# Attention and a softplus feed-forward on one core: block products in the first pass over d_ff for groups 4 and 5 too, and the softmax's scale after the product with v in the first group

## The chip, the core and the metric

One core of a Trainium2 chip runs the whole program. The metric is the device time of one execution in microseconds (us). The engines are TensorE (PE in the rows), VectorE (DVE), ScalarE (ACT), GpSimd (POOL) and SyncE (SP), which here does nothing but start DMAs.

## What is computed

```python
def _attn_ref(q, k, v):                       # B, H, S, D = 4, 8, 768, 64
    k_sum = k.reshape(B, H, nb, 32, D).max(axis=3)      # nb = 24 blocks of 32 keys
    v_sum = v.reshape(B, H, nb, 32, D).mean(axis=3)
    scores_l = scale * q @ k^T,   kept where abs(i - j) < 16
    scores_s = scale * q @ k_sum^T + log(32)
    a = softmax over [scores_l, scores_s]
    return a @ [v, v_sum]
def _moe_ref(x, w_in, w_out):                 # 3072 x 512, 512 x 2048, 2048 x 512
    h = x @ w_in
    return softplus(h) @ w_out
```

The output of the attention, with its heads side by side, is x. Everything is float32.

## The kernel before

**Tiling.** The 3072 tokens are 12 chunks of 256, and two chunks make a group of 512 tokens, so there are six groups, x = 0 to 5. d_ff = 2048 is 16 tiles of 128, f = 0 to 15. Phases follow one another: groups 0 to 4 with f = 0 to 7 (the first pass), group 5 with f = 0 to 15 at one stretch, then groups 4 to 0 with f = 8 to 15 (the second pass). A partial result of a group's first pass lies in DRAM until its second. The attention of group x + 1 is done while group x is in its first pass. Weights of f = 8 to 15 arrive, in the places of those of f = 0 to 7, while group 5 is worked on.

**Precision.** A float32 operand is split into a high and a low part that TensorE takes at its fast rate (float32r), and a product is three terms of those parts, so each product of 128 x 128 by some columns is three matmuls per tile of d_model.

**The two forms of x @ w_in.** `hidden(x, f)` is the plain one: four tiles of d_model by three terms, 12 matmuls of 512 columns into one PSUM bank. `hidden_pair(x, f)` does f and f + 1 together as a 2 x 2 block product with seven products in place of eight (tiles of d_ff by halves of the tokens by halves of d_model): each of the seven is 6 matmuls of 256 columns. It needs sums and differences of the blocks of w_in (`sums_of_weights`, buffers sw in places s0 to s3), sums and differences of the blocks of x (`prepare`: seven operands in places x0 to x6, of which x3 to x6 have one buffer), both banks that carry hidden values, and seven additions on VectorE. In the kernel before, `pairs = f0 > 0`: the second pass alone takes the pairs, and the first pass takes `hidden` on a group's x split whole (`prepare_whole`, `whole_x`).

Behind either form come, per f, ScalarE's softplus twice (gh, L1147, and the exact value, L1151), VectorE's rest gl (L1155), and 12 matmuls of 512 columns with w_out (L1162) into four banks.

**The first group's attention** has four blocks: chunk i (0, 1) by pair of heads hp (0, 2). Here they are called A (i 0, hp 0), B (i 1, hp 0), C (i 0, hp 2) and D (i 1, hp 2). For each, scores on TensorE (L629), mask and maximum on VectorE (L642), exp with sums on ScalarE (L650), the inverse of the sums (L657, L658), the scaling of the weights by it (`normalize`, on VectorE L663 for A and C, on ScalarE L666 for B and D), transposes on TensorE (L683), copies out of PSUM (L687), the product with v (L727), and from its bank the high and low parts of x (L757, L761). `keep_whole` adds these again later and writes them to DRAM for the second pass.

**Order.** Every operation is a task with an index, in the order in which the program declares them, and `SEQUENCE` says in which order the tasks are issued; a letter behind an index takes the task's second or third way (another engine). Each engine does its tasks in that order. In both kernels the tasks 3 to 42 are the warm-up, 43 to 63 loads and sums for the first batch, 153 to 245 the weights of f = 0 to 7, and 246 is the first product with w_in. Blocks A to D are the tasks 72 to 85, 86 to 99, 108 to 121, 122 to 135 before, and 72 to 88, 89 to 105, 114 to 130, 131 to 147 after the change.

## Time and profile before

| | |
|---|---|
| median of 3 runs | 631.66 us (630.81 to 633.7) |
| the profiled execution | 630.05 us |
| its span, first to last instruction | 628.3 us |
| mean granted TensorE clock | 0.983 of 2.4 GHz |
| HBM | 73.92 MB read, 27.26 MB written |

The span is what the trace shows; the profiled execution's own time is 1.75 us longer. A row of a group of instructions gives their line, engine, operation, tiles, shapes and count, then their busy time in us and the mean of one in ns, then the engine's idle time just before them and what ended it. Matmuls overlap one another, so the time that a row of them costs is read from start to start. "L1085" is a line of the program printed above.

### The profile page before, as it was taken

What the parts mean: (1) busy time and instruction counts of PE and PEld (TensorE: products, weight loads), DVE (VectorE), ACT (ScalarE), POOL (GpSimd) and SP (SyncE); (2) the same over time, 40 slices, a digit from 0 to 9 for tenths busy, and PEclk for the clock granted to TensorE, in tenths of its full rate; (3) what the DMA queues carried; (4) which work ended last, traced back from release to release, by engine and by line L of the source; (5) the groups of instructions that cost most, each with busy time, mean ns of one, the idle gap of its engine ahead of it and who ended that gap; (6) DMA issues with size and microseconds to landing.
All of it is one profiled execution on the core that took longest, in us unless ns stands there. A gap on an engine that the chain in (4) does not pass through costs nothing.

```text
span 628.3 us, 12022 instructions
## 1 busy us (share of the span) xinstructions
PE 609.2 (97%) x4452; PEld 508.9 (81%) x4452; DVE 388.0 (62%) x998; ACT 328.0 (52%) x809; POOL 162.0 (26%) x145
## 2 busy tenths in 40 slices
PE   8769999999999999999999999999999999999997
PEld 7557777788888878877888888899889899898995
DVE  5887997764457454535427979764557557655442
ACT  2898895965766676456526677441323122222220
POOL 3325435132213043002003443490111403002000
PEclk9868999999999999999999999999999999999999
DMA  9998887989998887885634632103122050030301
GB/s 303 265 272 268 254 264 233 262 261 231 272 263 253 259 268 220 254 236 158 212 116 155 222 127 84 34 34 118 51 76 78 17 185 1 35 100 1 104 32 67
DMA packets 88955, 104.39 MB, mean 166 GB/s; under 512 B 27489, under 2 KB 67009, under 8 KB 88129
## 3 DMA queue, kind: packets, MB, share of 16 engines
q1 hardware_dynamic: 88896, 103.62, 54.5%
q8 instruction: 35, 0.57, 0.4%
q14 instruction: 24, 0.19, 0.1%
HBM read 73.92 MB, written 27.26 MB: 161 GB/s over the span
## 4 chain that ended last, share of the span: by engine, by line
PE 85%; DMA 8%; SPq 3%; ACT 1%; DVE 1%; issue 1%; DVEq 0%; POOL 0%; POOLq 0%; ACTq 0%
PE po L1162 40%; PE ph L1045 21%; PE hx L1085 9%; PE hy L1085 7%; PE xo L727 3%; PE sc L629 3%; DMA raw<-w_in_dram 2%; DMA k<-kT_dram 2%; DMA squares<-tb 2%; PE warm L1236 2%; DMA kf<-kT_dram 1%; DMA q<-qT_dram 1%; DMA v<-v_hp_dram 1%; SPq L708 1%; SPq L523 1%
## 5 line engine op out<-in xcount | busy, mean ns | idle before, releaser
L1162 PE MATMUL po<-w,gh 128*128 128x512 f32 x768 | 204.2, 394 | 0.0
L1162 PEld LDWEIGHTS po<-w,gh 128*128 128x128 f32 x768 | 141.4, 188 | 30.6 <-issue 0.6
L1045 PE MATMUL ph<-xw,w 128*128 128x512 f32 x672 | 163.9, 395 | 2.1 <-DVE gl L1155 2.0
L1045 PEld LDWEIGHTS ph<-xw,w 128*128 128x128 f32 x672 | 125.6, 188 | 32.5 <-DVE gl L1155 2.8
L1162 PE MATMUL po<-w,gl 128*128 128x512 f32 x384 | 116.6, 397 | 0.0
L1162 PEld LDWEIGHTS po<-w,gl 128*128 128x128 f32 x384 | 70.9, 188 | 15.9 <-issue 0.5
L650 ACT ACTIVATE sp<-sp,nm 128x120 f32<-128x120 f32 x192 | 73.1, 382 | 5.9 <-DVE nm L642 5.7
L1147 ACT ACTIVATE gh<-hx 128x512 fp32r<-128x512 f32 x20 | 12.0, 599 | 114.9 <-DVE hx L1095 114.9
L948 POOL TENSOR_TENSOR t<-t,raw 128x1024 int32<-128x1024 int32 (+1 forms) x20 | 42.4, 2122 | 98.8 <-DVE t L934 28.4
L1155 DVE TENSOR_TENSOR gl<-ph,gh 128x512 fp32r<-128x512 f32 x56 | 38.0, 684 | 40.8 <-ACT ph L1151 39.3
L1147 ACT ACTIVATE gh<-ph 128x512 fp32r<-128x512 f32 x56 | 33.5, 598 | 53.4 <-PE ph L1045 48.5
L789 POOL TENSOR_TENSOR x<-r,x 128x512 fp32r<-128x512 f32 x18 | 24.5, 1370 | 82.0 <-ACT x L782 32.2
L642 DVE CUSTOM_DVE_ANT_0 sp<-sc,added 128x120 f32<-128x120 f32 x192 | 40.8, 277 | 4.9 <-PE sc L629 3.9
L663 POOL TENSOR_TENSOR sp<-sp,ss 128x960 f32<-128x960 f32 x10 | 18.4, 1843 | 87.6 <-DVE ss L658 62.8
L650 ACT ACTIVATION_READ_ACCUMULATOR sp<-sp,nm 128x1 f32 x192 | 36.0, 187 | 0.0
L1085 PE MATMUL hx<-x,sw 128*128 128x256 f32 x240 | 35.4, 283 | 0.0
L1085 PE MATMUL hx<-x,w 128*128 128x256 f32 x240 | 35.1, 282 | 0.0
L1085 PEld LDWEIGHTS hx<-x,w 128*128 128x128 f32 x240 | 32.8, 189 | 1.9
L696 DVE STREAM_TRANSPOSE tb<-sp 128x1024 f32<-128x1024 f32 x20 | 24.8, 1242 | 15.2 <-POOL sp L663 7.9
L1085 PE MATMUL hy<-x,sw 128*128 128x256 f32 x240 | 33.2, 282 | 0.0
L1151 ACT ACTIVATE ph<-ph 128x512 f32<-128x512 f32 x56 | 32.8, 591 | 0.0
L1085 PEld LDWEIGHTS hx<-x,sw 128*128 128x128 f32 x240 | 31.7, 189 | 0.5
(108 smaller groups left out, 821.6 us busy)
## 6 DMA issues: line engine op xcount, KB each, us to landing
squares<-tb SPq DMA_DIRECT2D x20, 512.0 KB
pT<-squares SPq DMA_DIRECT2D x80, 128.0 KB
raw<-w_out_dram SPq DMA_DIRECT2D x16, 512.0 KB
kf<-kT_dram SPq DMA_DIRECT2D x16, 384.0 KB
raw<-w_in_dram SPq DMA_DIRECT2D x6, 1024.0 KB
q<-qT_dram SPq DMA_DIRECT2D x20, 256.0 KB
raw<-r SPq DMA_DIRECT2D x20, 256.0 KB
part<-ob SPq DMA_DIRECT2D x10, 512.0 KB
```

Source lines behind the costliest of these rows:

```text
L629: nc.tensor.matmul(unit(g * NU + h * NPAIR + i)[r * QW:(r + 1) * QW, k0:k1], lhsT=q[rows, w * QW:(w + 1) * QW], rhs=k[rows], start=True, s ...
L642: nc.vector.tensor_tensor_reduce(out=sp()[:, n], in0=unit(n), in1=added()[:, kinds.index((lows[w], lows[w + 1]))], scale=-SCALE, scalar=FL ...
L650: nc.scalar.activation(sp()[:, n], sp()[:, n], AF.Exp, bias=nm()[:, n:n + 1], scale=-1.0, accum_out=ss()[:, n:n + 1],)
L696: nc.vector.transpose(out=tb().rearrange("p k (u q) -> p u k q", q=SQ), in_=tiles.sp().rearrange("p u (k q) -> p u k q", q=SQ),)
L789: engine.tensor_tensor(to(1), a(), to(0).bitcast(F32), op=ALU.subtract)
L948: nc.gpsimd.tensor_tensor(a, a, word(0, I32), op=ALU.add)
L1045: nc.tensor.matmul(ph(), lhsT=lhs(part, cc), rhs=xw[cc][0]()[:, xw[cc][1], a], start=cc == 0 and n == 0, stop=cc == NCC - 1 and n == 2,)
L1085: nc.tensor.matmul(to()[:, half], lhsT=lhs(wa, cc), rhs=of_x(xa)[:, cc * CH:(cc + 1) * CH], start=cc == 0 and m == 0, stop=cc == NG - 1 an ...
L1147: nc.scalar.activation(gh(), all_of(), AF.Softplus)
L1151: nc.scalar.activation(all_of(), all_of(), AF.Softplus)
L1155: nc.vector.tensor_sub(out=gl(), in0=all_of(), in1=gh().bitcast(F32))
L1162: nc.tensor.matmul(po[t](), lhsT=a()[:, t * P:(t + 1) * P], rhs=w2()[:, part, i2 * DM:(i2 + 1) * DM], start=f == f0 and i == 0, stop=f == ...
```

## The change

Two edits and a new order of issue.

1. Groups 4 and 5 (`SEVEN = 4` and up) take the pairs for f = 0 to 7 too. For that the sums of w_in of f = 0 to 7 are made once, after the declaration of group 4's attention, and both groups' x is prepared as seven operands. Group 5's f = 8 to 15 stay with eight products (`hidden_blocks`), taken from blocks of 256 columns: 24 matmuls of 256 columns per f, with one more block of x split for it (`single`). The sums for f = 8 to 15 no longer have a free place early; theirs is that of the sums of f = 0 to 7.
2. In the first group the scaling of the weights is gone. TensorE spreads the inverse sums over a bank (`spread`, eight matmuls of 128 columns against the identity), a copy brings them to SBUF, and VectorE multiplies the product with v by them (`scaled`). The result r goes to DRAM at once and is split by `prepare_whole`; `keep_whole` is gone. The raw values vn0 lie in the places r0 to r2.

```diff
 SEQUENCE = """
-0 3 4 162 43 1 5 6 51 7 44 8 9 10 11 12 13 14 15 16 17 18 19 20 21 22 23 24 25 26 27 28 29 30 31 32 33 153 45 47 68
-154a 158a 34 155 163a 64 46 52 156 53 55 164 2 157 165 167a 72 54 35 57 189 69 36 159 59 160a 161 49 73 48 37 86 313
-61 166 56 74 171 87 190 38 39 168 75 58 40 191 88 41 60 104 62 100 76a 172a 50 152 321a 180 192 176a 77 79 66 316 65
-173 174 63 67 169 42 78 108 71 175 80 170 70 177 314 315 185 194 101 109 89 312 193 110 122 123 81 324 208 198 181a
-103 90b 124 107 105 343 111 82 195 84 344 182 209a 91 102 136 106 196a 112a 346 183 199 184 92 93 94 95 325 83 213
-178a 197 85 342 113 125 326 372 345 96 186 210 211 114 179 351 212 138 115 116 98 117 99 97 376 126b 127 317 118 120
-327 214 200a 129 128 215a 130 354 137 217 131 373 246 218 380 328 329 134 330 140 132 121 141 355 133 320 119 135 201
...
+0 162 43 152 3 1 4 51 5 2 153 6 7 45 8 47 9 10 68 11 64 12 13 53 14 15 16 17 18 44 55 19 20 21 22 57 23 24 25 189 158a
+154a 26 27 163a 155 28 29 30 31 65 32 164 165 33 52 167 156 59 157 166 168 106 61 159 46 49 160 72 34 54 48 73 74 35
+110 89 190 56 194 191 161 169 66 58 192 60 50 62 69 70 313 36 76 90 63 193 195 171 91 78 37 114 38 67 71 208 314 112
+75 77 321a 172a 115 79 39 40 176a 170 131 80 196a 109 111 316 81 82 107 173 92 93 95 312 315 94 174 113 175 177 41 96
+116 197 83 108 148 132 180 209 227 210 211 97 98 99 85 118 87a 120 119 117 100 121 324 133 104a 325 343 42 122 372 181
+123 178 182 134 345 344 124a 135 88a 125 137 136 105a 138 102a 129a 86a 139 228a 130 183 351 151 342 229 346 213 326
+198 376 317 199 374 184 179a 140 185 141a 142 127a 103a 128 327 144a 150 146 145 246 354 147 255 378 212 149 318 328b
...
+1236 1249 1252 1119 1251 1250 1238 1142 1138 1143 1228 1229 1253 1120 1254a 1260 1261 1255a 884 1257 1262 1263 1546
+1258 1256 1264 1265a 1547a 1139 1259 1266 1269 1267 1270 1272 1268 1273 1275 1277 1271 1368 1278 1276 1281 1552 1282
...
@@ tile_long_short_attention__then__softplus_ffn_kernel
+    SEVEN = 4
@@ Sums.declare
+                if s_bufs:
+                    kf = buffer([P, S], F32, "kf", "t", T_BUFS, dynamic=True)
...
@@ Sums.declare_first_values
-                part = buffer([P, DM], F32, "vn0", tag="gh", bufs=NU)
+                part = buffer([P, DM], F32, "vn0", tag=f"r{i // 2}", bufs=2)
@@ attention
+        if not by_pe:
             (normalize, as before)
...
+        if by_pe:
+            r = block(2 * i + hp // NG)
+            xs = buffer([P, NG * CH], F32, "xs", "po", NT, psum)
+            def spread():
+                for n in range(NG * NU):
+                    g, h, w = n // NU, n % NU // NPAIR, n % NPAIR
+                    nc.tensor.matmul(
+                        xs()[h * D:(h + 1) * D, g * CH + w * P:g * CH + (w + 1) * P],
+                        lhsT=ss()[:, n:n + 1].broadcast_to([P, D]), rhs=ident(), start=True, stop=True,
+                    )
...
+            def brought(copy):
+                copy(out=r(), in_=xs())
...
+            def scaled():
+                nc.vector.tensor_tensor(r(), xo(), r(), op=ALU.mult)
...
-        if x and x < NX - 1:
+        if x and (x < NX - 1 or x >= SEVEN):
@@ prepare, n == 2
+            if x == NX - 1:
+                held = single[x] = buffer([P, 2, NG, CH], F32R, "x", tag="x0", bufs=2)
+                split(r12, lambda part: held()[:, part].rearrange("p g c -> p (g c)"), (held,), NG * CH)
@@ sums_of_weights
-        if f == HALF - 2:
-            begun.append(products[-1])
@@ hidden_blocks (new; hidden calls it when x >= SEVEN)
+        def product(i):
+            for hp in range(2):
+                of_x = blocks[i, hp][0]
+                for cc in range(NG):
+                    for n, (part, a) in enumerate(TERMS):
+                        nc.tensor.matmul(
+                            ph()[:, i * CH:(i + 1) * CH], lhsT=lhs(part, hp * NG + cc),
+                            rhs=of_x(a)[:, cc * CH:(cc + 1) * CH],
+                            start=hp == cc == n == 0, stop=hp == 1 and cc == NG - 1 and n == 2,
+                        )
@@ feed_forward
-        pairs = f0 > 0
+        plain = range(HALF, NF) if x == NX - 1 else range(HALF) if x < SEVEN else ()
+            pairs = not (f0 <= f < f1 and f in plain)
@@ the loops
-            attention(0, i, hp, tiles, True)
+            r, n = attention(0, i, hp, tiles, True), 2 * i + hp // NG
+            keep(0, n, r)
+            prepare_whole(0, n, {n: r})
...
+                if x >= SEVEN:
+                    prepare(x, n, r)
...
+            if x == SEVEN:
+                for f in range(0, HALF, 2):
+                    sums_of_weights(f)
```

In the two lines around 1253 of the new order, 1253 is group 5's last product with v, 1254a the copy of it, 1255 to 1265 the differences and splits that make its last operands, 1120 and 1139 products with w_out of group 4, and 1266 group 5's first product of half width.

## Rows read from the trace of the kernel before

**Rows 1.** The profile page, its first part: busy time, share of the span and number of instructions of each engine; and of its fourth part, the chain that ended last, the shares by engine.

```profile
PE 609.2 (97%) x4452; PEld 508.9 (81%) x4452; DVE 388.0 (62%) x998; ACT 328.0 (52%) x809; POOL 162.0 (26%) x145
...
PE 85%; DMA 8%; SPq 3%; ACT 1%; DVE 1%; issue 1%; DVEq 0%; POOL 0%; POOLq 0%; ACTq 0%
```

**Rows 2.** Busy time of each engine in stretches of the span. Columns: stretch, its length, then for TensorE (PE), its weight loads (PEld), VectorE (DVE), ScalarE (ACT) and GpSimd (POOL) the busy us and the number of instructions, the granted TensorE clock (1.00 is full), the DMA share, GB/s.

```profile
5.60:51.90 46.30, 36.81 (x554) 28.61 (x553) 37.77 (x137) 34.38 (x122) 16.08 (x14) 0.78 1.04 294
51.90:110.10 58.20, 55.50 (x452) 42.84 (x449) 50.23 (x145) 47.99 (x121) 23.86 (x16) 1.00 0.84 249
...
200.00:260.00 60.00, 60.00 (x531) 48.15 (x531) 29.32 (x123) 41.21 (x120) 15.29 (x17) 1.00 0.84 253
312.00:358.00 46.00, 46.00 (x227) 37.26 (x227) 28.36 (x43) 21.12 (x32) 13.12 (x9) 1.00 0.49 163
358.00:406.00 48.00, 48.00 (x210) 39.03 (x209) 41.29 (x51) 34.09 (x46) 18.75 (x10) 1.00 0.25 88
```

**Rows 3.** The same view in pieces of 10 us: at the start, in the last group's first pass, in the second pass.

```profile
40.00:50.00 10.00, 7.59 (x98) 6.42 (x98) 6.14 (x14) 10.00 (x35) 5.54 (x4) 0.54 1.08 282
350.00:360.00 10.00, 10.00 (x45) 8.11 (x44) 9.78 (x14) 4.62 (x5) 4.43 (x2) 1.00 0.60 210
...
440.00:450.00 10.00, 10.00 (x64) 9.00 (x63) 5.47 (x11) 3.20 (x6) 1.80 (x2) 1.00 0.24 80
```

**Rows 4.** What TensorE waited for from 50 us to the end, the longest in total: engine, line, releaser, us in total, times, longest.

```profile
PE ph L1045 <- DVE gl L1155: 2.0, 2, 1.2
```

**Rows 5.** The chain that ended last, in order of time (start, us, what), one piece of the first pass: the plain product (L1045), 12 instructions of 512 columns each.

```profile
140.00 2.77 PE ph L1045 x12
```

**Rows 6.** TensorE instructions in order of time (start, us, line, operation, output and inputs, shapes, count), one piece of the second pass: products of half width (L1085, six instructions of 256 columns each), then L1162.

```profile
409.02 0.88 PE L1085 MATMUL hx<-x,w 128*128 128x256 f32 x6
409.73 0.88 PE L1085 MATMUL hx<-x,sw 128*128 128x256 f32 x6
...
411.87 1.98 PE L1162 MATMUL po<-w,gh 128*128 128x512 f32 x8
413.69 1.10 PE L1162 MATMUL po<-w,gl 128*128 128x512 f32 x4
414.63 0.63 PE L1162 MATMUL po<-w,gh 128*128 128x512 f32 x2
```

**Rows 7.** Groups of instructions by line, engine and form, whole span: VectorE work on the products of half width (busy us, mean ns of one).

```profile
L1095 DVE TENSOR_TENSOR u<-hy,u 128x256 f32<-128x256 f32 x40 | 15.9, 421 | 14.1 <-PE hy L1085 13.9
...
L1095 DVE TENSOR_TENSOR hx<-hx,u 128x256 f32<-128x256 f32 x20 | 8.6, 431 | 7.3 <-PE hx L1085 6.8
...
L1105 DVE COPY p<-hx 128x256 f32<-128x256 f32 x12 | 5.1, 425 | 19.8 <-PE hx L1085 19.8
```

**Rows 8.** The same view: copying a product with v out of PSUM (L739), differences (L797), the high and the low half of an operand (L782, L789).

```profile
L789 POOL TENSOR_TENSOR x<-r,x 128x512 fp32r<-128x512 f32 x18 | 24.5, 1370 | 82.0 <-ACT x L782 32.2 <-ACT gh L1147 25.8 <-DVE x L782 24.0
...
L789 DVE TENSOR_TENSOR x<-r,x 128x512 fp32r<-128x512 f32 x17 | 13.6, 810 | 0.9 <-ACT x L782 0.9
...
L782 ACT CAST x<-r 128x512 fp32r<-128x512 f32 x21 | 12.8, 616 | 20.3 <-PE ph L1045 4.9 <-PE hy L1085 4.9 <-DMA r<-raw 4.8
...
L797 DVE TENSOR_TENSOR r<-r 128x512 f32<-128x512 f32 x10 | 6.9, 687 | 1.4 <-POOL x L789 1.2
...
L782 DVE CAST x<-r 128x512 fp32r<-128x512 f32 x14 | 5.8, 425 | 3.0 <-PE ph L1045 1.5 <-PE hx L1085 1.5
L739 DVE COPY r<-xo 128x512 f32<-128x512 f32 x8 | 5.5, 689 | 9.3 <-PE xo L727 9.3
```

**Rows 9.** The same view: the sums of the halves of w_in that the half-width products take (joined, combined, high half, low half).

```profile
L985 POOL TENSOR_TENSOR ws<-w 128x512 f32<-128x512 f32 x4 | 7.5, 1900 | 0.0
...
L1009 ACT CAST sw<-ws 128x1024 fp32r<-128x1024 f32 x3 | 3.2, 1055 | 1.8 <-POOL ws L996 1.8
...
L1016 DVE TENSOR_TENSOR sw<-ws,sw 128x1024 fp32r<-128x1024 f32 x2 | 2.6, 1302 | 0.0
...
L996 POOL TENSOR_TENSOR ws<-ws 128x256 f32<-128x256 f32 x1 | 0.7, 737 | 0.1
```

**Rows 10.** ScalarE in order of time, the start: the two scalings of softmax weights that it does there (L666), copies of transposed ones (L687) and casts of the results (L757).

```profile
31.96 2.38 ACT L666 ACTIVATE sp<-sp,ss 128x120 f32<-128x120 f32 x8
...
37.41 0.62 ACT L757 CAST xw<-xo 128x256 fp32r<-128x256 f32 x2
...
45.51 2.40 ACT L666 ACTIVATE sp<-sp,ss 128x120 f32<-128x120 f32 x8
...
49.36 1.06 ACT L687 COPY pT<-pt 120x512 f32<-120x512 f32 x2
```

**Rows 11.** TensorE in order of time, the start: transposes of the softmax weights (L683), products with v (L727), the first products with w_in (L1045).

```profile
46.82 1.96 PE L683 MATMUL pt<-ident,sp 128*120 128x128 f32 x8
...
50.66 1.34 PE L727 MATMUL xo<-pT,first 120*64 120x64 f32 x32
51.94 6.23 PE L1045 MATMUL ph<-xw,w 128*128 128x512 f32 x24
```

**Rows 12.** VectorE in order of time: the same operation on the same shape twice.

```profile
8.20 0.43 DVE L943 TENSOR_SCALAR raw<-raw 128x512 int32<-128x512 uint32 x1 [1.63 <-DMA raw<-w_in_dram]
...
11.74 1.52 DVE L943 TENSOR_SCALAR raw<-raw 128x512 int32<-128x512 uint32 x1
```

**Rows 13.** GpSimd in order of time, the same stretch.

```profile
11.62 1.34 POOL L948 TENSOR_TENSOR t<-t,raw 128x512 int32<-128x512 int32 x1 [5.30 <-DVE t L934]
```

## What the change should do to the time

> **What bounds the kernel now.** I read the page first: its busy shares and the shares of the chain that ended last. TensorE is busy 97% of the span and holds 85% of that chain, and DMA follows with 8% [rows 1]. Next the stretches. From 110 us on TensorE leaves no measurable gap in any stretch shown, while VectorE is at half load in the attention stage (29.32 of 60 us) and ScalarE at two thirds [rows 2]. Its waits say the same: after 50 us the largest sum is 2.0 us, in two places, on VectorE's gl [rows 4]. So for four fifths of the span a microsecond less of TensorE work is a microsecond less of time, if no new wait appears. The start differs. Up to the first product with w_in at 51.94 us [rows 11] TensorE is busy 36.81 of 46.30 us and at a mean clock of 0.78 [rows 2], and between 40 and 50 us ScalarE is busy 10.00 of 10 [rows 3]: there ScalarE's queue sets the pace. From 52 to 110 us VectorE is busy 50.23 of 58.20 and ScalarE 47.99 [rows 2], so this stretch is near three limits at once.
>
> **Block products for groups 4 and 5.** Twelve plain matmuls of 512 columns take 2.77 us [rows 5], so a pair of f takes 5.54. Six of 256 columns take 409.73 - 409.02 = 0.71 us [rows 6]; seven such products take 4.99 (at 0.713). Each pair saves 0.55. There are eight (f = 0 to 7 in two groups): 4.4 us off. The product with w_out is untouched.
>
> Group 5's f = 8 to 15 pay for it: 24 matmuls of 256 columns are four times 0.713, or 2.85 us against 2.77. Eight of them: 0.65 on. TensorE's net is **-3.75 us**. The form, 128 x 128 weights by 256 columns, is the one the trace has in the second pass, where TensorE has no gap [rows 3], so I put little uncertainty here: -4.4 to -3.
>
> **What else the pairs bring.** VectorE gets seven additions of about 0.42 to 0.43 us per pair, 2.95 in all, and a copy of 0.43 that ScalarE can also take [rows 7]: up to 13.5 us in each of the two groups. The extra sums of w_in cost per pair about 1.9 to join, four times 0.74 to combine on GpSimd, 1.06 on ScalarE and 1.30 on VectorE [rows 9]. The new order issues the first of them as group 3's first pass ends, where the similar stretch 200 to 260 us has VectorE at 29.32 and GpSimd at 15.29 of 60 [rows 2]. I cost them at nothing; without that cover one costs its pair up to 7 us once. Preparing x as seven operands is seven splits (0.62 high, 0.81 low) and four differences (0.69) [rows 8]; group 5 has an eighth split. The branch that puts kf and st elsewhere is never taken, since no sums exist when the last batch's are declared, and the dropped wait in sums_of_weights was for f = 6, which was never asked for: both nothing.
>
> **The change from group 4 to 5** gets a new wait. Operands 3 to 6 have one buffer each, and group 5's last block is multiplied with v just before. Counted in the order: behind task 1253 TensorE has 4 and 8 matmuls of L1162 (0.94 and 1.82 [rows 6]) and the first half-width product (0.71): 3.5 us until the second one wants its operand. VectorE and ScalarE need the copy 0.69, a difference 0.69, a high half and another difference 0.43 + 0.69 on VectorE beside the cast on ScalarE, a low half 0.81: 3.3 us [rows 8], just in time. The fourth product needs a difference and two more lows, 0.69 + 0.81 + 0.81: at 5.6 us, when TensorE gets there at 3.5 + 1.43 = 4.9. That is 0.7 us of idle time; behind it stand all six products left and the w_out products of group 4. From group 3 to 4 some 8 us of w_out work lie between the last product with v and the first pair, against a chain of the same length, so nothing. For the hand-overs between engines I round to **+1.0 us**. From below it is nothing; from above one whole chain laid bare, about 4.
>
> **The first group.** Removed: four scalings. The two on ScalarE take 2.38 and 2.40 us [rows 10] and lie ahead of the first product. Block D's exp ended at 37.41, where the casts of A follow, but its scaling began at 45.51: 8 us in a full queue. Counted in both orders up to task 246, ScalarE loses these two (4.8 us); six casts of about 0.33 give way to two copies and two casts of the same sum, and its decoding of weights is as long. VectorE loses two scalings and some lows and gets four products with the inverse, copies and casts; weights moved to later make that even. TensorE gets four spreads of eight matmuls of 128 columns in fp32; the like form, eight transposes, takes 1.96 us at the low clock there [rows 11]. Three fall into TensorE's 9.5 idle us [rows 2]; D's stands between the last product with v and the first with w_in. So the first product can start 4.8 - 1.96 = 2.8 us sooner. I take **-2.5 us**, since VectorE is close behind in the next stretch. Bounds: 4.8 sooner (spread hidden), or 1 later: if not the queue but D's own chain decides, it loses a scaling of 2.4 and gains spread 1.96, copy 0.69 and product 0.69. The DMAs that move (r written to DRAM at once, weights of f = 6 asked for before those of f = 2's w_out, q of block C ahead of the last keys) keep their bytes in SP's queue, which is full either way (share 1.04 [rows 2]); nothing. GpSimd's sums in keep_whole go, and lows of A and B come in their place.
>
> **Sum.** 630.05 - 3.75 - 2.5 + 1.0 = 624.8 for an execution like the profiled one. The median of the runs is 1.6 above that execution, so on their footing **626.4 us**, 0.8% less. About 0.5%, 3.2 us, is what a measurement of this kernel tells from no change.
>
> **One rule against it.** While GpSimd's 512-wide add ran from 11.62 to 12.96, a VectorE operation that takes 0.43 us alone took 1.52 [rows 12, 13]: 1.09 us lost in one meeting. The Trainium skill (SBUF — State Buffer, "SBUF: two separate sides") says why that would be: the port pair that VectorE and GpSimd share is an exclusive lock, held for a whole instruction. The trace agrees by that 1.09 us. By the row without meetings the sum stays 626.4; with them it is the first rival.
>
> **Rivals.**
> *VectorE becomes the bound in group 5's stretch (slower).* From 312 to 406 us it is busy 28.36 + 41.29 = 69.65 of 94 us [rows 2], and 9.78 of 10 in its fullest part [rows 3]. Added: 13.5 for four pairs and about 4 for the longer preparation, so 87.1 of 92.4 us (94 less TensorE's gain there, 1.6). 5.3 us are left. Each new meeting with GpSimd takes 1.09: five use that up, ten cost the whole gain as well, and if half of the 32 new operations meet one, 17.4 us, TensorE waits 12.1 us for additions and gl that come late: 626.4 - 1.0 + 12.1 = **637.5**. For it: the load. Against: VectorE was at 9.78 before and TensorE still had no gap, and weights and sums can go to ScalarE (34.09 of 48) or later. Chance 0.09.
>
> *The start gives its gain back.* From 52 to 110 us VectorE and ScalarE are above 82% [rows 2], the new order asks about as much of VectorE before the second group begins, and weights still have to be decoded. TensorE starts sooner, then waits. Only the products count: **628.9**. Chance 0.16, half of it above 628.5.
>
> *Hand-overs cost their upper bound*, 4 us in place of 1: **629.4**. For it: one buffer per operand. Against: the second pass changes groups on the same buffers, once between 440 and 450 us, and TensorE is at 10.00 there [rows 3]. Chance 0.08.
>
> *Everything hides*: 4.8 at the start, no wait: **623.1**. Chance 0.15.
>
> *The products don't get shorter*, if 256 columns between attention work run worse than in the second pass: nothing in the trace says so. With the other terms, 630. Chance 0.03.
>
> **Chances and range.** The forecast (624.5 to 628.4) has 0.49. Faster by over 0.5% means under 628.5: 0.49 + 0.15 + half of 0.16 is 0.72. The slow case is beyond 634.8: 0.09. What is left, half of 0.16, 0.08 and 0.03, is 0.19 within 0.5%. The range takes in the bound of the start (623.1, less 0.6 for scatter of the runs) and the cases up to 630, with 0.8 of scatter: 622.5 to 630.8. The slow case and the far tails stay out, about 0.2.
>
> **What would show it.** In the changed profile: 1176 instructions of 256 columns on the pairs' line (840 and 336), 192 on that of the new block products, and 384 plain ones of 512; six of 256 at 0.71 us in groups 4 and 5; no L666 before the first product and its start near 49.5 us; VectorE under 95% while group 5 runs and TensorE at 10.00 in those pieces; a gap near 1 us at group 5's first pair. Wrong would be: TensorE waiting on VectorE in 310 to 405 us, waits for operands at both changes of group, or a first product at 49 followed by idle time before 110.

## The result, and the profile after

The changed kernel takes 635.26 us (median of 20 runs, 630.62 to 641.03), the kernel before 630.63 (20 runs, 628.78 to 633.7): ratio 1.0066, 95% interval 1.0045 to 1.0087. It is slower by 0.7%, where 626.4 us and 0.8% faster was forecast. The profiled execution took 636.69 us, 1.4 above its median; its span is 634.9 us against 628.3. (The profiled execution of the kernel before took 630.05 us, so what follows explains 6.6 us, 2 more than lie between the medians.)

The page of the changed kernel, busy shares and the chain that ended last, against [rows 1]:

```profile
PE 610.6 (96%) x4756; PEld 518.1 (82%) x4756; DVE 425.8 (67%) x1088; ACT 342.6 (54%) x821; POOL 190.9 (30%) x160
...
PE 74%; DMA 8%; SPq 7%; DVE 4%; ACT 4%; issue 2%; POOL 0%; DVEq 0%; POOLq 0%; ACTq 0%
```

TensorE's share of the chain falls from 85% to 74%; SyncE's queue, VectorE, ScalarE and "issue" take what it lost. Stretches of the changed kernel, columns as in [rows 2]; the first two end at the first product with w_in and at group 1's first one:

```profile
5.60:49.70 44.10, 36.66 (x587) 28.14 (x586) 31.48 (x126) 25.34 (x87) 12.00 (x12) 0.92 1.01 272
49.70:116.10 66.40, 58.70 (x483) 44.49 (x482) 55.79 (x160) 55.63 (x151) 28.13 (x16) 0.97 0.88 246
200.00:260.00 60.00, 59.13 (x499) 47.32 (x498) 37.69 (x121) 41.73 (x118) 22.65 (x20) 1.00 0.79 230
312.00:358.00 46.00, 46.00 (x327) 41.18 (x322) 34.51 (x68) 25.41 (x39) 9.48 (x9) 1.00 0.55 188
...
70.00:80.00 10.00, 8.01 (x71) 6.21 (x69) 6.87 (x24) 7.52 (x11) 4.91 (x2) 0.83 1.05 271
...
360.00:370.00 10.00, 10.00 (x53) 8.50 (x53) 9.65 (x15) 8.15 (x11) 4.96 (x3) 1.00 0.56 191
```

The first product comes 2.2 us sooner (49.7 against 51.9), but the stretch behind it takes 66.4 us where it took 58.2, so group 1 begins 6.0 us later (116.1 against 110.1). From 312 to 400 us TensorE has no gap. TensorE in order of time in the changed kernel: the first products; then waits for queries, keys and transposed softmax weights ("squares"); then one place in group 3's first pass and one in group 5's stretch:

```profile
49.70 1.65 PE L1095 MATMUL ph<-xw,w 128*128 128x512 f32 x6
51.27 1.05 PE L639 MATMUL sc<-k,q 64*64 64x120 f32 x32
52.25 5.01 PE L1095 MATMUL ph<-xw,w 128*128 128x512 f32 x18
58.45 0.73 PE L1213 MATMUL po<-w,gh 128*128 128x512 f32 x2 [1.19 <-ACT gh L1198]
60.28 0.50 PE L1213 MATMUL po<-w,gl 128*128 128x512 f32 x1 [1.09 <-DVE gl L1206]
...
69.38 0.64 PE L639 MATMUL sc<-k,q 64*64 64x120 f32 x16 [0.97 <-DMA q<-qT_dram]
71.77 1.08 PE L639 MATMUL sc<-k,q 64*64 64x120 f32 x16 [1.75 <-DMA k<-kT_dram]
...
92.91 1.15 PE L738 MATMUL xo<-pT,v 120*64 120x64 f32 x32 [2.09 <-DMA squares<-tb]
...
263.65 1.65 PE L1095 MATMUL ph<-xw,w 128*128 128x512 f32 x6 [1.86 <-ACT r L774]
...
336.57 0.88 PE L1135 MATMUL hx<-x,sw 128*128 128x256 f32 x6
337.28 1.59 PE L1135 MATMUL hy<-x,sw 128*128 128x256 f32 x12
```

Six of 256 columns take 337.28 - 336.57 = 0.71 us in group 5 as forecast. Between the first product and group 1, waits for transfers come to 0.97 + 1.75 + 2.09 = 4.8 us; in the kernel before there was one, of 0.5. The waits at 58 and 60 us are for the first softplus. ScalarE in order of time shows why (its later lines are two more scalings of softmax weights):

```profile
30.51 0.69 ACT L944 ACTIVATE t<-raw 128x512 f32<-128x512 f32 x1 [3.38 <-DMA raw<-w_in_dram]
...
36.70 0.59 ACT L760 COPY r<-xs 128x512 f32<-128x512 f32 x1 [5.02 <-PE xs L753]
...
54.06 2.43 ACT L677 ACTIVATE sp<-sp,ss 128x120 f32<-128x120 f32 x8
56.51 1.28 ACT L1198 ACT_TABLE_LOAD   x1
57.80 0.60 ACT L1198 ACTIVATE gh<-ph 128x512 fp32r<-128x512 f32 x1
...
66.30 2.38 ACT L677 ACTIVATE sp<-sp,ss 128x120 f32<-128x120 f32 x8
...
97.76 2.40 ACT L677 ACTIVATE sp<-sp,ss 128x120 f32<-128x120 f32 x8 [2.17 <-DVE ss L668]
```

and in the kernel before the same first softplus and the one scaling of that stretch, and on TensorE one block's scores ahead of the first product and the one wait for a transfer behind it:

```profile
57.04 0.60 ACT L1147 ACTIVATE gh<-ph 128x512 fp32r<-128x512 f32 x1
...
79.39 2.40 ACT L666 ACTIVATE sp<-sp,ss 128x120 f32<-128x120 f32 x8 [1.80 <-DVE ss L658]
```

```profile
48.72 2.02 PE L629 MATMUL sc<-k,q 64*64 64x120 f32 x32
...
94.32 0.64 PE L629 MATMUL sc<-k,q 64*64 64x120 f32 x16 [0.54 <-DMA k<-kT_dram]
```

ScalarE idles 3.38 and 5.02 us early, for a transfer and for the new spread, so its queue no longer sets the pace of the start by itself; it is behind afterwards, and reaches the first softplus 0.8 us later than before although TensorE is 2.2 us ahead. At 54.06, 66.30 and 97.76 it scales softmax weights of group 1's blocks, three times where before it did so once; before, GpSimd had the others.

**Ledger of the two profiled executions.** I gave each TensorE instruction to its task by the order of issue and took, for each product with w_in or w_out, the time from its start to the next one's start (its spacing). A spacing above 267 ns for 512 columns (133 for 256) is cut to 233 (116), and the rest counts as a wait.

| us | before | changed | difference |
|---|---|---|---|
| first product with w_in | 51.9 | 49.7 | -2.2 |
| products with w_in | 255.4 | 251.4 | -4.0 |
| products with w_out | 265.1 | 266.9 | +1.8 |
| waits between products | 10.0 | 19.0 | +9.0 |
| all else behind the first product | | | +2.2 |
| end of TensorE | 623.4 | 630.2 | +6.8 |

One block's scores of group 1 (0.98 us) now stand behind the first product and make part of "all else". About 1 us of the 9.0 is no waiting: from 73.4 to 75 us products start 412 to 427 ns apart, in the one stretch behind the first product whose granted clock is low (0.83 from 70 to 80 us; 1.00 from 51.9 to 110.1 us in the kernel before [rows 2]). TensorE had just waited 0.97 and 1.75 us.

### The profile page after: what moved, and what is told of

The parts are those of the page before. It is cut to its first block, busy times and chain, and to the rows that moved or that the text cites. A ratio compares the mean times of both kernels' runs of the same rounds, so it can differ in the third digit from the quotient of the medians.

```text
span 634.9 us, 12720 instructions
## 1 busy us (share of the span) xinstructions
PE 610.6 (96%) x4756; PEld 518.1 (82%) x4756; DVE 425.8 (67%) x1088; ACT 342.6 (54%) x821; POOL 190.9 (30%) x160
## 3 DMA queue, kind: packets, MB, share of 16 engines
q1 hardware_dynamic: 88896, 103.62, 54.9%
## 4 chain that ended last, share of the span: by engine, by line
PE 74%; DMA 8%; SPq 7%; DVE 4%; ACT 4%; issue 2%; POOL 0%; DVEq 0%; POOLq 0%; ACTq 0%
PE po L1213 36%; PE hx L1135 12%; PE hy L1135 9%; PE ph L1095 8%; PE xo L738 3%; PE ph L1069 3%; PE sc L639 3%; DMA raw<-w_out_dram 2%; ACT sp L660 2%; DMA st<-v_hp_dram 1%; SPq L533 1%; DMA vn<-v_hp_dram 1%; SPq L719 1%; SPq L507 1%; SPq L516 1%
## 5 line engine op out<-in xcount | busy, mean ns | idle before, releaser
L1213 PE MATMUL po<-w,gl 128*128 128x512 f32 x384 | 116.3, 396 | 1.1 <-DVE gl L1206 1.1
L1095 PE MATMUL ph<-xw,w 128*128 128x512 f32 x384 | 95.8, 397 | 1.9 <-ACT r L774 1.9
L1095 PEld LDWEIGHTS ph<-xw,w 128*128 128x128 f32 x384 | 71.1, 188 | 20.3 <-ACT r L774 2.3
L1135 PE MATMUL hx<-x,w 128*128 128x256 f32 x336 | 49.0, 282 | 0.3 <-DVE gl L1206 0.3
L1135 PE MATMUL hx<-x,sw 128*128 128x256 f32 x336 | 49.0, 282 | 0.0
L1135 PEld LDWEIGHTS hx<-x,w 128*128 128x128 f32 x336 | 45.8, 189 | 3.4 <-DVE gl L1206 0.7
L1135 PE MATMUL hy<-x,sw 128*128 128x256 f32 x336 | 45.1, 281 | 0.0
L1135 PEld LDWEIGHTS hx<-x,sw 128*128 128x128 f32 x336 | 44.2, 189 | 0.6
L1135 PEld LDWEIGHTS hy<-x,sw 128*128 128x128 f32 x336 | 42.3, 188 | 0.3
L1206 DVE TENSOR_TENSOR gl<-ph,gh 128x512 fp32r<-128x512 f32 x40 | 26.9, 681 | 20.0 <-ACT ph L1202 18.2
L1145 DVE TENSOR_TENSOR u<-hy,u 128x256 f32<-128x256 f32 x56 | 21.8, 420 | 14.0 <-PE hy L1135 13.9
```

The lines of the kernel that those rows point to most:

```text
L1095: nc.tensor.matmul(ph(), lhsT=lhs(part, cc), rhs=xw[cc][0]()[:, xw[cc][1], a], start=cc == 0 and n == 0, stop=cc == NCC - 1 and n == 2,)
L1135: nc.tensor.matmul(to()[:, half], lhsT=lhs(wa, cc), rhs=of_x(xa)[:, cc * CH:(cc + 1) * CH], start=cc == 0 and m == 0, stop=cc == NG - 1 an ...
L1145: DVE, dve(CH), lambda: nc.vector.tensor_tensor(out(), a(), b(), op=op), reads, [write],
L1206: nc.vector.tensor_sub(out=gl(), in0=all_of(), in1=gh().bitcast(F32))
L1213: nc.tensor.matmul(po[t](), lhsT=a()[:, t * P:(t + 1) * P], rhs=w2()[:, part, i2 * DM:(i2 + 1) * DM], start=f == f0 and i == 0, stop=f == ...
```

## Experiments

**The change cut in two at group 2.** Each task was put in the order of one kernel up to group 2's first product and in that of the other behind it.

```diff
 run h1_new_start_only
-    SEVEN = 4
+    SEVEN = NX
 SEQUENCE: changed kernel's up to "first product of group 2", then that of before
 run h2_block_products_only
-        if by_pe:
+        normalize as before
 SEQUENCE: that of before up to "first product of group 2", then the changed kernel's
```

> The new form of the first group in the changed kernel's own order, up to the first product of group 2; from there the order of the kernel before, without block products for groups 4 and 5. Theory A (the first group's new start and the order around it lose the time): the first product near 49.7 us, group 2 at about 168.7 instead of 164.0 us, the rest as before, so some 4.5 us slower than before, about 635 us. Theory B (the block products, or the order of the later groups, lose it): group 2 no later than 164 us and the whole at 628 to 631 us.

> The other half: the order of the kernel before and its first group up to the first product of group 2, from there the changed kernel's order with block products for groups 4 and 5. Theory A: group 2 starts at 164.0 us as before, the products give back 3.75 us, and the stalls that the changed kernel has behind that point (9.4 us against 5.1 before) take some 4 us of it: 627 to 631 us. Theory B: 633 us or more, since all of the loss is then in here.

Measured: 639.66 us (1.0126, interval 1.0094 to 1.0158) and 638.81 (1.0119, 1.0095 to 1.0143), against 630.96 for before. The first fits neither theory. The second is what theory B expected, but both halves lose more than the whole, so the cut itself costs. In h2_block_products_only, VectorE and TensorE behind the cut:

```profile
172.67 1.81 DVE L358 TENSOR_REDUCE ks<-kf 128x24 f32<-128x768 f32 x2 [5.52 <-DMA kf<-kT_dram]
...
177.59 0.80 PE L1087 MATMUL ph<-xw,w 128*128 128x512 f32 x1 [5.23 <-DVE gl L1198]
```

A load of keys that the cut makes late holds a maximum on VectorE for 5.52 us, gl stands behind it in the same queue, and TensorE waits 5.23 us for gl. This pair of runs therefore says nothing of the two edits. It shows how dear a late transfer is at the head of an in-order queue. The Trainium skill (TensorE: Matmul & The Clock Gate, "Architectural detail: the array is 16× 32×32, not 1× 128×128") calls VectorE's queue strictly first in, first out; the 5.52 us agree.

**The new form in the old order, and with block products behind it.**

```diff
 run e4_new_form_old_order (run b4_new_form_and_products: the same, then the changed order from group 2 on)
-    SEVEN = 4
+    SEVEN = NX
-        ss = buffer([P, NG * NU], F32, "ss")
+        ss = buffer([P, NG * NU], F32, "ss", bufs=4)
 SEQUENCE: that of before; the spread right behind each block's product with v
```

> The first group's new form alone, set into the order of the kernel before with as few tasks moved as possible (the widening of the row of factors right behind the block's product with v), and with four buffers for the exponentials' sums in place of two; no block products for groups 4 and 5. If the form itself costs (six more small instructions a block, the later use of the factors): 633 us or more. If what costs is the order in which the changed kernel takes this stretch, or its wait for the two buffers: the first product 1 to 3 us sooner than 51.9 and the whole at 627 to 630 us.

> The start of the run e4_new_form_old_order, followed from group 2 on by the changed kernel's order with block products for groups 4 and 5. If the two edits add up without the changed kernel's start, the time is that of e4_new_form_old_order plus that of h2_block_products_only less that of the kernel before: 624 to 629 us. If it is 634 us or more, the start is not what makes the changed kernel slow.

Measured: 631.70 us (1.0010, 0.9992 to 1.0028), as before and between the two cases expected; and 637.18 (1.0098, 1.0072 to 1.0124), which has the cut at group 2 in it again (TensorE waits 4.23 us for gl there, and the products behind that wait start 427 ns apart for some 5 us). In the first the products with w_in start at 54.9 us, 3.0 later than before. ScalarE shows the reason:

```profile
49.23 0.58 ACT L755 COPY r<-xs 128x512 f32<-128x512 f32 x1 [2.93 <-PE xs L748]
50.58 0.71 ACT L827 CAST xw<-r 128x256 fp32r<-128x256 f32 x2 [0.76 <-DVE r L762]
```

A block now passes from the product with v through spread, copy, product and cast, three engines in turn, where one cast took it out of PSUM before. In this order the new form gives no earlier start. That the whole still came out even has a cause that I had not thought of: its products took 518.2 us where those of before, the same in number and kind, took 520.6. The larger ss had moved most operands and the hidden values to 64 bytes off the weights modulo 128; half-width products took 113 to 120 ns there, 116.0 in the mean, and 118 to 120 before.

**64 bytes more ahead of the buffers of operands and hidden values**, in either kernel. A product reads its weights and, against them, an operand of x or a hidden value; these runs move the second kind of buffer and nothing else:

```diff
     psum = ctx.enter_context(tc.tile_pool(name="psum", bufs=2, space=bass.MemoryType.PSUM))
+    work.tile([P, 16], F32, name="pad", tag="pad", bufs=1)
```

> The kernel before, with 64 unused bytes per partition ahead of the operands, hidden values and scratch buffers, so that these lie 64 bytes further on against the weights; order and work unchanged. Theory (the spacing of the products depends on where their two operands lie to each other: in the run e4_new_form_old_order half-width products whose operand had moved by 64 bytes took 113 to 114 ns, the others 119 to 120): 840 half-width products at 113.5 in place of 118.9 ns, 4.5 us, and some 2 us on the products with w_out: 624 to 626 us. Rival (that spacing came from the time at which they ran, not from the place): 630 to 632 us.

> The same 64 bytes in the changed kernel, order and work unchanged. Theory of the place: 1176 half-width products 5 ns shorter each, 6 us, and 2 to 3 us on the products with w_out (232.3 ns each in the changed kernel, 230.8 before): 626 to 629 us against 635. Rival: 634 to 636 us.

Measured: 629.61 us (0.9986, 0.9965 to 1.0007) and 628.65 (0.9986, 0.9966 to 1.0005). The changed kernel is thus shorter by 5.0 us with 64 unused bytes (by the ratios 1.0066 and 0.9986, since it ran in other rounds; its median is 6.6 lower), as the theory said. Its products take 513.1 us in place of 518.3. In the kernel before neither case came: half-width products fall to 116.3 ns, but those with w_out rise from 230.8 to 232.4, 520.3 in all. With these 64 bytes the two kernels have the same ratio: the loss is gone, to within 1.8 us, and no gain stands in its place, though the changed kernel's products are 7.2 us shorter.

**Is it the softmax's order on ScalarE?** Exponentials ahead with six buffers for the sums; the six buffers alone; and three tasks taken out of the way of what TensorE waits for.

```diff
 runs c1_exp_ahead and c2_six_buffers_only
-        ss = buffer([P, NG * NU], F32, "ss")
+        ss = buffer([P, NG * NU], F32, "ss", bufs=6)
 run c1_exp_ahead, order on ScalarE
-pT A, ks, mag w_in, pT A, brought A, pT B, pT B, exp C, ..., pT C, exp D
+pT A, ks, exp C, mag w_in, pT A, exp D, brought A, pT B, pT B, ..., pT C
 run d1_scalar_queue
-normalize group 1's first block on ScalarE; mask of its second block, low half of the first hidden tile; exp x5, copy of x4's product with v
+normalize group 1's first block on VectorE; low half of the first hidden tile, mask of its second block; copy of x4's product with v, exp x5
```

> The changed kernel with six buffers for the sums of the exponentials in place of two, and the exponentials of the first group's third and fourth block moved ahead on ScalarE: the third ahead of the magnitudes of a tile of w_in (from 38.7 us to about 27), the fourth ahead of the copy of the first block's spread factors (to about 33.5); the score maxima of the fourth block move with it. Buffers stay where they were within 128 bytes. Theory A (the first group's start loses the time, because these exponentials stand behind the spread of an earlier block and ScalarE idles from 27 to 37 us): group 1 begins at 111 to 113 us in place of 116.1 and the whole takes 629 to 632 us. Rival (the stretch waits for transfers or weights instead): 634 us or more.

> The changed kernel with the six buffers alone, its order unchanged. If the order already written down holds the third block's exponential back (it stands behind the copies of the second block's transposed exponentials), nothing moves: 634 to 636 us. If the two buffers held it: 632 us or less.

> The changed kernel with three tasks moved, buffers where they were: the normalization of group 1's first block goes from ScalarE (2.43 us at 54.1, ahead of the first softplus) to VectorE; the low half of the first hidden tile goes on VectorE ahead of the score maxima of group 1's second block; the copy of group 4's product with v goes on ScalarE ahead of group 5's first exponential. Theory D (the changed order puts long softmax work on an in-order engine ahead of what TensorE waits for): the stalls at 55.7 and 58.5 us (1.36 and 1.47 us) and at 259.8 us (2.05 us) go, 630 to 632 us against 635. Rival (such a stall only makes room for the next wait, on transfers): 634 to 636 us.

Measured: 632.27 us (1.0045, 1.0024 to 1.0066), 634.62 (1.0058, 1.0033 to 1.0084) and 634.26 (1.0083, 1.0056 to 1.0111). In c1_exp_ahead the third block's exponential comes 11.7 us sooner (27.00 against 38.71) and the first product still at 50.3, so the exponentials do not hold the start back; its time lies between the two cases, and its difference from c2_six_buffers_only (0.8 us by the ratios) is within the noise. In c2_six_buffers_only the time stayed where it was, as expected if the order held the exponential. In d1_scalar_queue the wait of 1.86 us at 263.65 is gone, and the first group's third hidden tile begins 1.3 us sooner (59.97 against 61.30); other waits follow, 1.39 us for gl up to 64.30, 1.59 for keys up to 70.95, 1.25 up to 75.82, and 0.99 up to 278.77. Its rival was right: room made by one wait goes to the next.

**Where the buffers lie.**

```diff
 runs k0_all_at_256 (c2_six_buffers_only and this), a0_after_32_bytes_on, p2_before_32_bytes_on (the kernel and this)
+    const.tile([P, 8], F32, name="pad0", tag="pad0", bufs=1)
     ident = Buffer(order, const, [P, P], F32, "ident")
 run d2_queue_exp_160: moves of c1 and d1, six buffers, and
+    work.tile([P, 48], F32, name="pad", tag="pad", bufs=1)
 run k1_queue_exp_192_of_0: d2 and the 32 bytes
 runs p3_before_best_layout, k2_best_layout: 32 and 192 bytes, six buffers, and gaps around gh and gl
```

> The run c2_six_buffers_only with 32 unused bytes ahead of all buffers, so that weights, operands and hidden values all begin at a multiple of 256 bytes in their partition (before: 224 bytes behind one). Theory E (the products' spacing depends on the place of both operands modulo 256 bytes, relative to each other): as in that run, 228.5 ns for full and 119.6 ns for half width, 633 to 635 us. Rival (it depends on whether a row of an operand begins at a multiple of 64 bytes): spacing down to 222 ns or less and 115 ns or less, 624 to 628 us.

> The three moves of d1_scalar_queue, the exponentials of c1_exp_ahead with its six buffers, and 192 unused bytes ahead of operands and hidden values, so that these begin 160 bytes and the weights 224 bytes behind a multiple of 256. Theory E: half-width products at 114 to 116 ns, products with w_out at 229 to 230 ns, some 6 us under the changed kernel's; theory D: 3 to 5 us more; together 624 to 628 us. If neither the place nor the queue matters: 632 us as c1_exp_ahead.

> The run d2_queue_exp_160 with 32 more unused bytes ahead of all buffers: the weights begin at a multiple of 256 bytes, operands and hidden values 192 bytes behind one. Theory E (only the distance of the two counts): the time and the spacings of d2_queue_exp_160 within 1 us. Rival (a beginning at a multiple of 64 bytes counts): shorter by 3 us or more.

> The changed kernel with 32 unused bytes ahead of all buffers and nothing else: each buffer then begins at a multiple of 64 bytes, and the distances between them stay, so that by theory E the products keep their spacing (518.3 us in all). Theory F (what the run k0_all_at_256 won over c2_six_buffers_only, 8 us with the same order and the same spacing of the products, comes from the beginning at a multiple of 64 bytes, in the stretch before 225 us that waits for transfers): 626 to 630 us. Rival (it came from something else that those two runs do not share): 634 to 636 us.

> The same 32 bytes in the kernel before. Theory F, if it holds whatever the order: 3 to 6 us shorter than before, 624 to 627 us, and the change costs some 4 us in this layout too. If the kernel before does not wait for its transfers and only the changed one does: 629 to 631 us, and the two kernels then differ by less than 2 us or the changed one is ahead.

> The kernel before with its buffers placed by theory E: weights at a multiple of 256 bytes, operands 192 bytes behind one (half-width products at 115 to 116 ns), hidden values at a multiple of 256 as the weights (products with w_out at 228.5 ns), by unused bytes and six buffers for the sums of the exponentials. Products 516 us in place of 520.6: 625 to 627 us; with theory F 3 us less. Rival (spacing follows something else): 629 to 631 us.

> The run k1_queue_exp_192_of_0 with its hidden values moved to a multiple of 256 bytes as the weights, operands 192 bytes behind one as there. Theory E: products with w_out at 228.5 in place of 230.0 ns, products 510 us in all: 624 to 626 us. If the changed kernel has kept the gain of its block products and of its earlier start, it is 4 to 6 us under the run p3_before_best_layout; if what it gained is lost in new waits, within 2 us of it.

Distances are those of an operand or hidden value from the weights, modulo 256 bytes; products in us as in the ledger, spacing in ns.

| run | operands | gh, gl | w_out spacing | half width | products | median us, ratio (interval) |
|---|---|---|---|---|---|---|
| before | 0, 128 | 0, 128 | 230.8 | 118.8 | 520.6 | 630.63 |
| p2 | 0, 128 | 0, 128 | 230.8 | 118.8 | 520.5 | 628.20, 0.9969 (0.9948 to 0.9990) |
| changed | 0, 128 | 128, 128 | 232.3 | 118.7 | 518.3 | 635.26, 1.0066 |
| a0 | 0, 128 | 128, 128 | 232.3 | 118.6 | 518.2 | 629.93, 1.0003 (0.9982 to 1.0024) |
| c2 | 0 | 0, 0 | 228.5 | 119.6 | 513.9 | 634.62, 1.0058 |
| k0 | 0 | 0, 0 | 228.5 | 119.6 | 514.0 | 626.38, 0.9945 (0.9925 to 0.9965) |
| d2 | 192 | 192, 192 | 230.1 | 115.5 | 511.9 | 626.81, 0.9947 (0.9925 to 0.9969) |
| k1 | 192 | 192, 192 | 230.0 | 115.4 | 511.7 | 626.88, 0.9947 (0.9928 to 0.9967) |
| k2 | 192 | 0, 0 | 227.9 | 117.5 | 512.1 | 626.98, 0.9940 (0.9917 to 0.9963) |
| p3 (before) | 192 | 0, 0 | 227.9 | 117.6 | 517.4 | 625.05, 0.9921 (0.9890 to 0.9952) |

Five pairs with equal distances (before and p2, changed and a0, c2 and k0, d2 and k1, k2 and p3) have equal spacings, four of them with all large buffers moved by 32 bytes, the last with different orders: how the buffers lie to each other counts, not where they begin. In k0_all_at_256 the spacing was that of theory E and the time that of its rival; spacing by multiples of 64 is out, and the time is what theory F is about. p2's time fell between its two cases; k2 came 1 us above its range and 1.9 above p3, so by its second case the changed kernel's gain is lost in waits.

Theory E failed in one point: with gh and gl moved (k2), half-width products took 117.5 ns, not 115.4, though their operands had kept their distance. Single products show that the distance of the two operands does not settle the spacing. All operands lie at 192 in d2_queue_exp_160 and in k2_best_layout, yet in the first 734 of 1360 half-width products took at most 115.5 ns and the others mostly some 118, several in a row of one kind; in the second 84 did. The means in the table are mixtures of the two; what chooses between them is open. In d2_queue_exp_160 six products of the same tiles took 331.05 - 330.34 = 0.71 us at one place and 341.54 - 340.86 = 0.68 at another:

```profile
330.34 0.87 PE L1136 MATMUL hx<-x,sw 128*128 128x256 f32 x6
331.05 1.58 PE L1136 MATMUL hy<-x,sw 128*128 128x256 f32 x12
...
340.86 0.84 PE L1136 MATMUL hx<-x,sw 128*128 128x256 f32 x6
341.54 1.52 PE L1136 MATMUL hy<-x,sw 128*128 128x256 f32 x12
```

By groups of lines (busy us, mean ns of one; matmuls overlap, so these means are longer than the spacings), one group of products with w_out and one of half width, of c2_six_buffers_only:

```profile
L1213 PE MATMUL po<-w,gh 128*128 128x512 f32 x768 | 203.6, 393 | 1.2 <-ACT gh L1198 1.1
...
L1135 PE MATMUL hx<-x,sw 128*128 128x256 f32 x336 | 49.5, 283 | 0.0
```

of d2_queue_exp_160:

```profile
L1214 PE MATMUL po<-w,gh 128*128 128x512 f32 x768 | 204.7, 395 | 0.2 <-DVE w L982 0.2
...
L1136 PE MATMUL hx<-x,sw 128*128 128x256 f32 x336 | 47.9, 278 | 1.0 <-DVE u L1146 1.0
```

and of the changed kernel:

```profile
L1213 PE MATMUL po<-w,gh 128*128 128x512 f32 x768 | 207.4, 398 | 1.2 <-ACT gh L1198 1.2
...
L1135 PE MATMUL hx<-x,sw 128*128 128x256 f32 x336 | 49.0, 282 | 0.0
```

The second effect is that of the 32 bytes, which put every large buffer on a multiple of 64 and leave the spacing alone. Stretch 20 to 50 us, the last two columns being the DMA share and GB/s: of before, p2_before_32_bytes_on, the changed kernel, a0_after_32_bytes_on, c2_six_buffers_only and k0_all_at_256 in turn.

```profile
20.00:50.00 30.00, 21.16 (x323) 17.14 (x326) 23.61 (x85) 27.40 (x94) 10.85 (x7) 0.68 1.03 266
```

```profile
20.00:50.00 30.00, 20.01 (x343) 15.40 (x344) 27.22 (x98) 29.29 (x104) 11.29 (x9) 0.89 0.90 268
```

```profile
20.00:50.00 30.00, 22.97 (x401) 19.09 (x402) 21.55 (x97) 18.72 (x66) 8.70 (x7) 0.89 0.97 236
```

```profile
20.00:50.00 30.00, 25.46 (x442) 20.25 (x441) 24.27 (x102) 22.26 (x80) 8.72 (x7) 0.94 0.96 261
```

```profile
20.00:50.00 30.00, 24.12 (x407) 18.99 (x406) 23.47 (x100) 20.18 (x68) 8.72 (x7) 0.94 1.04 246
```

```profile
20.00:50.00 30.00, 24.89 (x442) 18.91 (x440) 24.70 (x102) 22.45 (x79) 8.72 (x7) 1.00 0.97 268
```

GB/s by share of the engines rise from 258 to 298, 243 to 272 and 237 to 276: a byte costs 11 to 14% less DMA engine time in that stretch. By the ratios the time follows by 1.9 us in the kernel before, by 4.0 in the changed one (5.3 by the medians, of different rounds), by 7.1 from c2 to k0 (8.2), and not at all from d2 to k1, though there too the share falls (1.00 at 249 GB/s, 0.92 at 252). Theory F holds for the first three pairs; what decides how much of it reaches the time is not settled. In the changed kernel the waits for transfers between the first product and group 1 fall from 4.8 us to 0.7 (a0):

```profile
PE sc L640 <- DMA k<-kT_dram: 0.7, 1, 0.7
```

But a_pad_after_64_bytes_on has none of them either, with buffers that begin 32 bytes behind a multiple of 64, so the multiple of 64 is not the only thing that ends them.

**The change cut in two at group 1's first product with w_out**, where the two orders differ by nine tasks, with the 32 bytes in both:

```diff
 run g1_products_from_group_1
 SEQUENCE: that of before up to "first product with w_out of group 1", then the changed kernel's
 run g2_first_group_only
-    SEVEN = 4
+    SEVEN = NX
 SEQUENCE: the changed kernel's up to there, then that of before
```

> The run p2_before_32_bytes_on up to the first product with w_out of group 1 (its first group and order as before, group 1 from 108.6 us), and from there the changed kernel's order with block products for groups 4 and 5. Buffers lie as in p2_before_32_bytes_on. If the block products carry their gain to the end (4.1 us on the products, against some 2.9 us more waits in the changed order between groups 1 and 4): 626 to 628 us. If the waits around them take all of it: 628 to 630 us, as p2_before_32_bytes_on or above.

> The run a0_after_32_bytes_on up to the first product with w_out of group 1 (from 110.2 us, 1.6 us later than in p2_before_32_bytes_on), and from there the order of the kernel before without block products for groups 4 and 5. Buffers lie as in a0_after_32_bytes_on, where the products with w_out take 1.7 us more in all. If the first group's new form is what costs: 630 to 633 us, the sum of the two terms above p2_before_32_bytes_on. If it costs nothing: 628 to 629 us, and g1_products_from_group_1 is then the slow one.

Measured: 629.79 us (0.9992, 0.9968 to 1.0015) and 631.46 (1.0013, 0.9985 to 1.0042), against 628.20 with neither edit (p2) and 629.93 with both (a0). g1's products take 516.7 us, 3.8 less than p2's, and its waits 16.0 in place of 8.9: its second case, the waits take the gain. g2 met its first case. Neither edit alone is faster than p2; how the 1.7 us of the whole divide between them is below what these intervals resolve. The waits do divide. With the changed start alone (g2) there are 8.8 us of them up to group 1 and 5.4 behind it, with the block products and their order alone (g1) 4.6 and 11.4, in p2 4.4 and 4.5. Both profiled executions were longer than their medians, by 4.4 and 2.6 us, so the sizes are rough.

**Waits at four placements.** Changed kernel less kernel before, by the ledger, in us; the time by the ratios, with its uncertainty. The two of a pair have the same unused bytes; gh still lies elsewhere in the two, except in the last pair, where k2's order has the moves of c1 and d1 in it.

| pair | products | waits up to group 1 | waits behind | time |
|---|---|---|---|---|
| changed, before | -2.3 | +5.8 | +3.3 | +4.2 (1.3) |
| a0, p2 (32 bytes) | -2.3 | +3.8 | +3.1 | +2.1 (1.9) |
| a_pad, p1 (64 bytes) | -7.2 | +4.3 | +3.4 | 0.0 (1.8) |
| k2, p3 (32 and 192 bytes, gaps) | -5.3 | +3.8 | +3.7 | +1.2 (2.4) |

Placement alone moves the changed kernel's products by up to 6.6 us (518.3 against 511.7 in k1). The waits are 6.9 to 9.0 us longer at each of the four.

## Why the prediction was wrong

**Block products: right.** 1176 instructions of 256 columns on the pairs' line, 192 block products and 384 plain ones stand in the changed trace, six of 256 at 0.71 us, and products with w_in fall by 4.0 us (3.75 forecast).

**"The product with w_out is untouched": wrong.** Its instructions are the same, but the change places gh 128 bytes from the weights modulo 256 in place of 0, and 1149 of them take 1.8 us more. The sum had no term for where buffers lie. Nor had it one for the multiple of 64: with 32 unused bytes in each kernel the difference falls from 4.6 us to 629.93 - 628.20 = 1.7 (by the ratios 1.0003 and 0.9969, each uncertain by 0.0021, 2.1 us with 1.9 of uncertainty). With 64 in each, 4.2 us by the ratios fall to none, uncertain by 1.8. So the loss hangs on the layout: the fall to none is clear of noise, that to 2.1 is not by itself. That the change gains nothing does not hang on it: at none of four placements is the changed kernel resolvably faster.

**The first group, -2.5 us: the step that failed.** The earlier first product came (2.2 us), but the number owes something to luck: ScalarE had done 9.0 us less by then, not 4.8, VectorE 6.3 less where "even" was reckoned, and one block's scores of group 1, 2.02 us at 48.72 before, had moved behind it. What failed is the step from an earlier first product to an earlier end. The sum carried the 2.5 us through and charged only 1.0 us for waits, at the change from 4 to 5; it put the transfers that move at nothing and counted ScalarE's and VectorE's work only as far as task 246. The runs showed in its place:
- *Work put off.* By group 1's first product ScalarE has been busy 25.34 + 55.63 = 81.0 us, before 34.38 + 47.99 = 82.4 [rows 2]: of the 4.8 removed, 1.4 are left, as the new order gives ScalarE two more scalings of group 1 (2.4 us each) than before. It has done 9.0 us less by the first product and does 7.6 more behind it. VectorE's work shifts likewise (37.77 to 31.48, then 50.23 to 55.79).
- *Waits.* Between the first product and group 1 TensorE idles 66.40 - 58.70 = 7.7 us, before 58.20 - 55.50 = 2.7. In the traced execution 4.8 of the 7.7 are for transfers, against 0.5; the first softplus, 2.3, is nearly matched by 2.0 us of waits for gl before [rows 4]. At all four placements this stretch has 3.8 to 5.8 us more waits, and they come with the changed start (g2), not with the block products (g1).

That the waits follow from the work put off is argued from these sums. Taking ScalarE's scaling out of the way (d1) removed the wait for gh and gained no time, and what makes single transfers late was not tried.

The prediction named the sign itself, "a first product at 49 followed by idle time before 110". Its rival "The start gives its gain back" had this with chance 0.16 and the words "TensorE starts sooner, then waits", but stopped at nothing gained; the stretch lost another 6.0 us. With the 32 bytes too, a0 is at 47.2 us for its first product, 3.7 ahead of p2, and 1.6 behind it at group 1 (110.2 against 108.6).

**Waits between groups, +1.0 at the change from 4 to 5: wrong place.** TensorE shows no wait there (336.57). A wait for a buffer came some 70 us earlier: the bank of group 4's product with v is copied out behind group 5's exponential on ScalarE, and group 3's last tile waits 1.86 us for that bank at 263.65. It stands in a0 (2.0) too. Behind group 1's first product the changed kernel has some 3 us more of waits than the kernel before (7.6 us in a0, 4.5 in p2).

**VectorE as the bound, 637.5 us: wrong mechanism, though nearest in time.** From 312 to 400 us VectorE reaches 9.65 of 10 us and TensorE has 10.00. The Trainium skill's rule of the exclusive port pair (SBUF — State Buffer, "SBUF: two separate sides") speaks of a cost that in that stretch never reached TensorE.

## What to carry to other kernels

Count the work that stands ahead of a point and behind it on the slowest in-order engine: an earlier start with that work only put off can give the time back. A sum that takes work off a busy engine needs a term for the waits that the new order brings; here it was 6.9 to 9.0 us against products shorter by 2.3 to 7.2. Two kernels whose buffers lie elsewhere differ by that too, so compare an edit at equal placement, or at several, before the edit is blamed or praised. Here placement alone is worth more than the edit: the kernel before with its buffers moved takes 625.05 us and beats both kernels.

## What was not expected of the hardware

The mean spacing of products changes with how their buffers lie to each other: full-width products with w_out 227.9 to 232.4 ns, half-width ones 115.4 to 119.6. I reckoned distances modulo 256 bytes; no run tests another period, and the distance of a product's own two operands is not the whole rule (d2 and k2). Transfers with all large buffers on multiples of 64 bytes, in place of 32 bytes behind one, cost 11 to 14% less DMA engine time from 20 to 50 us in three pairs and 9% less in a fourth. And all runs with the changed kernel's start show TensorE waiting over 1 us at the first group's scores for nothing that the profile names, which no run with the start of before does; of the changed kernel (us in total, times, longest):

```profile
PE sc L639 <- issue: 4.6, 2, 3.0
```

It ranged from 1.4 to 5.1 us in these runs. What it is was not tried.
